# One kernel, 116 small stages in a new order: projections first, the last inverse by quarters, weights*v in two halves, u regrouped on VectorE

## The chip, the cores and the metric

The kernel runs on one core of one Trainium2 chip. The metric is the device time of one execution in microseconds (us). Most executions of a kernel agree within about 1.5%. A run that is over 1.5% above the fastest of its kernel counts as slow; such runs are left out of the comparisons. Two sets of numbers appear: the times of repeated runs, and the profile of one run of each kernel, whose span is about 2 us shorter than its time.

## The reference, cut to what matters

Two independent parts share the core; their outputs stand side by side.

```python
def _A_ref(x, wqkv, wo):                       # part A: sliding dilated attention, S=2048, D=640
    qkv = (x @ wqkv)...                        # q, k, v; 32 heads of 20
    idx = pos[:, None] - 2 * arange(8)         # each position sees 8 earlier ones, step 2
    logits = einsum("bhsd,bhswd->bhsw", q, kg) * scale
    attn = softmax(logits)
    o = einsum("bhsw,bhswd->bhsd", attn, vg)   # weights * v
    return o @ wo
def _B_ref(u, A, B, C, log_dt, Dskip):         # part B: a long convolution, L=2048, D=640, N=192
    P = exp(dt * A * l)                        # powers; K is their sum over N
    K = einsum("dn,dnl,dn->dl", C, P, dt * B).real
    y = irfft(rfft(u, 2L) * rfft(K, 2L))[:L]   # one transform per channel
    return y + u * Dskip
return concatenate([a, b], axis=-1)            # the bodies are abridged
```

## The kernel before

The stages, with the letters that the change gives them: `q k v` are the projections (five slices each, of 20 matmuls), `L` the logits of one half of a block of 512 positions, `N` the softmax normalisation, `A` weights*v for one of five slices, `O` the output projection. For part B, `G` makes the generators (sines and cosines) of the powers, `M` one of five tables with the convolution kernel made of it, `U` regroups u, `f g x y` are an FFT (u's first step, the table's first step, the second step with the product, the transform back), `S` the skip product, and `I` the last inverse. `R` frees the projections' memory and opens the FFT's.

```python
ORDER = "L0 V0 M1 F0 L1 M2 F1 V1 L2 M3 F2 V2 M4 F3 L3 F4 S012 I012 V3 S34 I34"

# in front of ORDER, fixed: generators, table 0, k, q, u, v
gens(tc, pools, ta, wi, 0, 1, dst0, done0); batch(1, 3); batch(3, 5)
make(0)
for ct in range(5): a.proj("k", ct)
for ct in range(5): a.proj("q", ct)
for i in range(4):
    us = att.tile([128, 16, 160], bf16, name="us", tag="p2")            # one buffer
    ... four loads on the GpSimd queue
    for h in range(2):
        uc = att.tile([128, NCH, 8, 32], bf16, name="uc", tag="prod", bufs=2)
        nc.gpsimd.tensor_copy(out=uc[:], in_=us[:, 8*h:8*h+8].rearrange("p l (c t) -> p c l t", c=NCH))
        nc.gpsimd.dma_start(out=Ud[:, :, s]..., in_=uc[:]...)
for ct in range(5): a.proj("v", ct)

# one projection slice: TensorE into two PSUM buffers, ScalarE moves each out
for sc in range(4):
    ps = self.psp.tile([128, 512], f32, name="ps_p", tag="a", bufs=2)
    for kt in range(5): nc.tensor.matmul(ps[:], ...)
    nc.scalar.copy(out=st[:, sc], in_=ps[:])

# weights * v: one multiply, one buffer
p2 = p.tile([128, 2, 4, PB], bf16, name="p2", tag="p2")
V.tensor_tensor(out=p2[:], in0=windows(v...), in1=self.at[b][:]..., op=A.mult)
ps = self.psp.tile([128, PB], f32, name="ps_o", tag="l", bufs=2)
for u2 in range(2):
    for d in range(4):
        nc.tensor.matmul(ps[32*d:32*d+32], lhsT=G4, rhs=p2[:, u2, d], start=(u2 == 0), stop=(u2 == 1), ...)
# (cut: everything else)
```

The softmax here doesn't subtract the row's maximum and nothing guards it: scores larger than these inputs give would overflow.

## Time and profile before

459.38 us is the median of three runs (459.04 to 460.1).

The first lines of the page of the kernel before: the span; busy time of TensorE (PE), its weight loads, VectorE (DVE), ScalarE (ACT) and GpSimd (POOL); then the busy share of TensorE and VectorE, and the clock granted to TensorE, each in 40 slices of the span, in tenths.

```profile
span 457.8 us, 13032 instructions
...
PE 352.9 (77%) x5560; PEld 232.3 (51%) x5560; DVE 350.9 (77%) x521; ACT 253.6 (55%) x485; POOL 82.2 (18%) x149
...
PE   1863646196999766599898979988799799998680
...
DVE  1499947998799984568999798989889944576443
...
PEclk9999978878899965579998988999599978999896
```

No engine is full: the two busiest stand at 77%. Where they idle is told by the windows view. Each row is a stretch: from and to in us, its length, then busy us of PE, PEld, DVE, ACT, POOL, the granted clock, the DMA share and GB/s.

```profile
0.00:97.00 97.00, 49.09 (x222) 20.44 (x223) 72.22 (x159) 64.34 (x123) 36.36 (x62) 0.90 0.76 190
97.00:156.00 59.00, 55.07 (x716) 28.51 (x717) 54.08 (x96) 31.30 (x54) 7.13 (x10) 0.94 0.54 183
156.00:200.00 44.00, 27.24 (x669) 16.70 (x663) 27.49 (x27) 9.74 (x17) 8.81 (x23) 0.57 0.67 189
200.00:360.00 160.00, 146.69 (x2547) 108.78 (x2546) 144.40 (x185) 98.05 (x193) 15.13 (x30) 0.93 0.38 115
360.00:416.00 56.00, 49.01 (x1052) 37.59 (x1046) 35.86 (x39) 35.11 (x68) 4.40 (x8) 0.91 0.52 173
416.00:458.00 42.00, 25.81 (x372) 20.27 (x370) 16.80 (x20) 15.09 (x34) 10.33 (x16) 0.85 0.63 139
```

The middle (200 to 360) is about 91% full on both engines. At 156 to 200 both are near 62% at once, and the granted clock is 0.57. In that stretch VectorE, from 160.5 on, has only the first attention block to work on. Its timeline there (start, length, line, operation, output<-inputs; in brackets the idle time before it and what ended that) shows a chain that goes back and forth between the engines and the transfers:

```profile
174.15 0.96 DVE L448 RECIPROCAL rc<-ps_n 128x128 f32<-128x128 f32 x1 [4.48 <-PE ps_n L445]
...
179.69 1.22 DVE L456 TENSOR_TENSOR attn<-attn,ps_r 128x1024 bf16<-128x1024 bf16 x1 [3.98 <-PE ps_r L455]
...
184.39 2.29 DVE L467 TENSOR_TENSOR p_1859<-vb,attn 128x4096 bf16<-128x4096 bf16 x1 [1.15 <-PE ps_o L471]
189.19 2.29 DVE L467 TENSOR_TENSOR p_1876<-vb,attn 128x4096 bf16<-128x4096 bf16 x1 [2.51 <-DMA vb<-vd]
```

The waits of TensorE (who waited at which line, for whom; us in total, times, longest) show one large item: the projections wait 30.3 us for ScalarE, which is busy with the generators' sines.

```profile
PE ps_p L400 <- ACT st L401: 30.3, 8, 9.8
```

At the end, three pieces of the chain that ended last (start, length, what): the transform back ends at 423.5, and after it evictions, an output projection and a store follow one another up to 457.8.

```profile
424.12 3.08 ACT ysb L685 x8
...
432.56 4.27 PE ps_op L482 x20
...
442.63 5.10 DMA out_dram<-ud
```

### The profile page before, as it was taken

Reading aid. Unit: us, or ns where it says so; the run is one execution under the profiler, and the core shown is the slowest. Engines: PE = TensorE matmul, PEld = TensorE weight load, DVE = VectorE, ACT = ScalarE, POOL = GpSimd, SP = SyncE. Lnnn points to the kernel's source line nnn. Section 1 sums busy time; section 2 is a strip of 40 time slices with the busy share of each in tenths; the row PEclk is TensorE's granted clock in tenths of the full one; section 3 lists DMA queues with packets and bytes.
Section 4 is the critical chain, followed back from the end, with each engine's and each line's share of the span. In section 5 each row is a group of like instructions: output and inputs, shape, how many; then the busy total and the mean of one; then the engine's idle time right before and its main releaser. Section 6 shows DMA issues by size and latency. Waiting matters only on the chain.

```text
span 457.8 us, 13032 instructions
## 1 busy us (share of the span) xinstructions
PE 352.9 (77%) x5560; PEld 232.3 (51%) x5560; DVE 350.9 (77%) x521; ACT 253.6 (55%) x485; POOL 82.2 (18%) x149
## 2 busy tenths in 40 slices
PE   1863646196999766599898979988799799998680
PEld 0520212045444344166587737667476576776470
DVE  1499947998799984568999798989889944576443
ACT  1869646984455401176771775673276734786540
POOL 8235640000500020310000220000210000010232
PEclk9999978878899965579998988999599978999896
DMA  8999656435664293774051543241443108583687
GB/s 180 259 212 231 184 157 221 133 133 168 187 246 153 90 298 91 186 226 133 21 210 50 141 128 130 105 163 50 103 154 124 62 4 311 203 229 95 157 204 113
DMA packets 64822, 71.50 MB, mean 156 GB/s; under 512 B 29744, under 2 KB 55664, under 8 KB 63868
## 3 DMA queue, kind: packets, MB, share of 16 engines
q1 hardware_dynamic: 57740, 54.89, 40.6%
q0 software_dynamic: 5664, 14.96, 13.0%
q10 hardware_dynamic: 1360, 0.82, 0.7%
q8 instruction: 43, 0.70, 0.7%
q14 instruction: 15, 0.12, 0.1%
HBM read 43.72 MB, written 24.02 MB: 148 GB/s over the span
## 4 chain that ended last, share of the span: by engine, by line
PE 37%; DVE 11%; ACT 6%; issue 3%; DMA 2%; POOL 0%; DVEq 0%; POOLq 0%; ACTq 0%
PE ps_ia L351 9%; PE ps_k L280 7%; PE ps_op L482 4%; PE ps_s L304 3%; ACT S L338 3%; PE ps_o L471 3%; DVE Yf L341 2%; PE ps_l L436 1%; DVE krtmp L223 1%; ACT ysb L685 1%; DMA vb<-vd 1%; DVE Ytab L223 1%; DMA out_dram<-ud 1%; DVE prod L434 1%; PE ps_r L455 1%
## 5 line engine op out<-in xcount | busy, mean ns | idle before, releaser
L400 PE MATMUL ps_p<-xT,w_309 128*128 128x512 bf16 x100 | 36.2, 526 | 35.9 <-ACT st L401 30.3
L434 DVE TENSOR_TENSOR prod<-qb,kb 128x2048 bf16<-128x2048 bf16 x40 | 47.5, 1221 | 19.1 <-PE ps_l L436 17.2
L280 PE MATMUL ps_k<-Ytab,Xtab 128*20 128x33 bf16 (+1 forms) x2560 | 51.9, 245 | 11.9 <-issue 10.6
L465 POOL DMA_DIRECT2D vb<-vd x40 | 22.2, 558 | 201.8 <-DVE p_4181 L467 43.8
L280 PEld LDWEIGHTS <-Xtab 128*20 128x20 bf16 (+1 forms) x2560 | 45.5, 126 | 20.8 <-issue 18.0
L401 ACT CAST st<-ps_p 128x512 bf16<-128x512 f32 x60 | 34.7, 580 | 24.7 <-PE ps_p L400 24.2
L400 PEld LDWEIGHTS <-w_309 128*128 128x128 bf16 x100 | 12.1, 123 | 59.2 <-issue 50.6
L351 PE MATMUL ps_ia<-cEA,Yf 128*128 128x256 bf16 x320 | 41.0, 295 | 0.2 <-DVE Yf L341 0.2
L351 PEld LDWEIGHTS <-Yf 128*128 128x128 bf16 x320 | 33.3, 106 | 9.3 <-DVE Yf L341 3.3
L353 ACT CAST Z<-ps_ia 128x512 bf16<-128x512 f32 x40 | 23.4, 585 | 22.7 <-PE ps_ia L351 22.6
L482 PE MATMUL ps_op<-wo,oT 128*128 128x320 bf16 x160 | 30.1, 322 | 5.3 <-ACT oT L473 4.0
L223 DVE TENSOR_TENSOR Ytab<-Ytab 128x2688 bf16<-128x2688 bf16 (+3 forms) x25 | 30.7, 1228 | 2.4 <-DMA Ytab<-Gdram 2.1
L336 PEld LDWEIGHTS <-cT 128*64 128x64 bf16 x640 | 22.9, 113 | 16.2 <-issue 14.4
L223 DVE TENSOR_TENSOR krtmp<-Ytab 128x2688 bf16<-128x2688 bf16 (+3 forms) x25 | 29.7, 1190 | 0.2
L282 ACT CAST Kd<-ps_k 128x363 bf16<-128x363 f32 (+1 forms) x15 | 6.8, 453 | 40.8 <-PE ps_k L280 40.8
L341 DVE TENSOR_TENSOR Yf<-S 128x1024 bf16<-128x1024 bf16 x40 | 25.7, 687 | 3.4 <-ACT S L338 3.4
L223 DVE TENSOR_TENSOR krtmp<-Xtab,Xg 128x768 bf16<-128x768 bf16 (+2 forms) x40 | 26.2, 655 | 0.6
L223 DVE TENSOR_TENSOR Xtab<-Xtab,Xg 128x768 bf16<-128x768 bf16 (+2 forms) x40 | 25.7, 650 | 0.3
L214 ACT ACTIVATE cs<-ph 128x768 bf16<-128x768 int32 x22 | 17.7, 842 | 13.0 <-DMA Gdram<-cs 13.0
L400 PE MATMUL ps_p<-xT,w_311 128*128 128x512 bf16 x100 | 24.5, 406 | 0.0
L436 PE MATMUL ps_l<-prod,cGs 128*32 128x512 bf16 x160 | 18.9, 424 | 7.1 <-DVE prod L434 7.1
L482 PEld LDWEIGHTS <-oT 128*128 128x128 bf16 x160 | 14.6, 101 | 18.9 <-ACT oT L473 10.5
(452 smaller groups left out, 745.6 us busy)
## 6 DMA issues: line engine op xcount, KB each, us to landing
vb<-vd SPq DMA_DIRECT2D x40, 128.5 KB, 3.0
vb<-vd POOLq DMA_DIRECT2D x40, 128.5 KB, 3.7
Gdram<-cs SPq DMA_DIRECT2D x24, 192.0 KB, 3.8
HB<-k_HB SPq DMA_DIRECT2D x2, 2048.0 KB, 8.4
kb<-kd SPq DMA_DIRECT2D x4, 657.5 KB
us<-in_B_u_dram POOLq DMA_DIRECT2D x16, 160.0 KB, 6.2
Udram<-uc POOLq DMA_DIRECT2D x8, 320.0 KB, 5.0
kd<-st SPq DMA_DIRECT2D x5, 512.0 KB, 3.8
```

The source lines that it names most:

```text
L223: V.tensor_tensor(out=o[0], in0=Y[0], in1=gr, op=A.mult)
L280: MM(ps[32 * g:32 * g + 20, i, :], lhsT=X[rows, part % 2, :, col + t0 + i], rhs=Y[rows, :, part % 2, col + t0 + i], start=(part == 0 and i ...
L336: nc.tensor.matmul(ps[64 * dd:64 * dd + 64, kk, r], lhsT=T[:, k, r, :], rhs=A1[:, k, :, 64 * dd:64 * dd + 64], start=(kk == 0 and r == 0), ...
L341: V.tensor_tensor(out=Yf[:, 2 * i:2 * i + 2, :, 32 * b:32 * b + 32], in0=K, in1=u.unsqueeze(1).to_broadcast([128, 2, 16, 32]), op=A.mult)
L351: nc.tensor.matmul(ps[:, jj].rearrange("p l r d -> p (l r d)"), lhsT=Yf[:, q, 2 * jq + jj, :], rhs=C["EA"][:, q, :], start=(jj == 0 and q ...
L353: nc.scalar.copy(out=Z[:, :, :, 4 * jq:4 * jq + 4].rearrange("p l r (j d) -> p (l r) j d", d=2), in_=ps[:].rearrange("p j l r d -> p (l r) ...
L400: nc.tensor.matmul(ps[:], lhsT=w[:, kt, 128 * ct:128 * ct + 128], rhs=self.xT[:, kt, 512 * sc:512 * sc + 512], start=(kt == 0), stop=(kt = ...
L401: nc.scalar.copy(out=st[:, sc], in_=ps[:])
L434: V.tensor_tensor(out=pr[:], in0=q[:, ct].unsqueeze(1).to_broadcast([128, 4, PB]), in1=windows(k[:, ct, 2 * u2:2 * u2 + PB], 4, 4), op=A.mult)
L436: nc.tensor.matmul(ps[32 * g:32 * g + 32], lhsT=C["Gs"][:, ct, :], rhs=pr[:, g, :], start=(ct == 0), stop=(ct == 4), tile_position=(0, 32 ...
L465: (nc.sync if g % 2 else nc.gpsimd).dma_start(out=v[32 * g:32 * g + 32], in_=self.vd[:, 4 * dg:4 * dg + 4, PB * b + 4 * g:PB * b + 4 * g + ...
L482: nc.tensor.matmul(ps[:], lhsT=self.oT[b][:, t, 128 * x:128 * x + 128], rhs=self.wo_sb[:, t, 320 * eh:320 * eh + 320], start=(t == 0), sto ...
```

## The change

The intent is to fill idle time. No matmul and no eviction is removed. (1) The coarse stages become 116 small ones, and the written order is new: q and k first, the fixed front dissolved, the eight pieces of the last inverse (four quarters for each of two batches) spread over the tail. (2) weights*v becomes two multiplies of half the size in two buffers, so that TensorE can start on the first half. (3) The eight copies that regroup u go from GpSimd to VectorE, and u's tile is halved and gets two buffers. Core of the diff, with the mere splitting of functions into stages cut:

```diff
-ORDER = "L0 V0 M1 F0 L1 M2 F1 V1 L2 M3 F2 V2 M4 F3 L3 F4 S012 I012 V3 S34 I34"
+ORDER = "q4 q1 q2 q3 q0 G0 G1 k0 k4 k2 v4 k1 k3 M0 U1 U0 v2 U2 U4 v0 v3 U5 U7 U6 v1 L0 L1 U3 N0
+         A0 A1 A2 A3 A4 G3 R0 L2 L3 N1 M1 O2 O1 O0 O3 f0 g0 x0 f1 A5 M2 A6 A7 g1 y0 x1 M3 A8 A9
+         ... f4 A15 A16 A17 A18 A19 g4 x4 I0 I1 S4 S5 y4 I2 S6 I4 I3 S7 O13 O14 I5 O12 I6 O15 I7"
...
-        p2 = p.tile([128, 2, 4, PB], bf16, name="p2", tag="p2")
-        V.tensor_tensor(out=p2[:], in0=windows(v[:, :, 0:PB], 2, 2), in1=..., op=A.mult)
         for u2 in range(2):
+            p2 = p.tile([128, 4, PB], bf16, name="p2", tag="p2", bufs=2)
+            V.tensor_tensor(out=p2[:], in0=v[:, :, 2 * u2:2 * u2 + PB], in1=..., op=A.mult)
...
-        us = att.tile([128, 16, 160], bf16, name="us", tag="p2")
+        us = att.tile([128, 8, 160], bf16, name="us", tag="p2", bufs=2)
...
-            nc.gpsimd.tensor_copy(out=uc[:], in_=us[:, 8 * h:8 * h + 8].rearrange("p l (c t) -> p c l t", c=NCH))
+        V.tensor_copy(out=uc[:], in_=us[:].rearrange("p l (c t) -> p c l t", c=NCH))
```

More of the change, by code (lines that the diff above doesn't have):

```diff
@@ L19 @@
 CW = 192
-ORDER = "L0 V0 M1 F0 L1 M2 F1 V1 L2 M3 F2 V2 M4 F3 L3 F4 S012 I012 V3 S34 I34"
+ORDER = "q4 q1 q2 q3 q0 G0 G1 k0 k4 k2 v4 k1 k3 M0 U1 U0 v2 U2 U4 v0 v3 U5 U7 U6 v1 L0 L1 U3 N0 A0 A1 A2 A3 A4 G3 R0 L2 L3 N1 M1 O2 O1 O0 O3 f0 g0 x0 f1 A5 M2 A6 A7 g1 y0 x1 M3 A8 A9 O6 O5 O7 L4 L5 N2 y1 O4 f2 g2 x2 M4 S0 S1 S2 S3 A10 A11 y2 f3 g3 A12 A13 A14 O9 O11 x3 O8 y3 L6 O10 L7 N3 f4 A15 A16 A17 A18 A19 g4 x4 I0 I1 S4 S5 y4 I2 S6 I4 I3 S7 O13 O14 I5 O12 I6 O15 I7"
 MAGIC = 12582912.0
@@ L118, in partB_prep @@
     W = NCH * CW
-    nat01 = ap.tile([128, 4, NCH, CW], bf16, name="nat01", tag="p2")
-    nat2 = ap.tile([128, 2, NCH, CW], bf16, name="nat2", tag="prod", bufs=2)
-    nat = [nat01[:, a] for a in range(4)] + [nat2[:, a] for a in range(2)]
+    nat = []
+    for tag in ("p2", "p2", "prod"):
+        nt = ap.tile([128, 2, NCH, CW], bf16, name="nat", tag=tag, bufs=2)
+        nat += [nt[:, 0], nt[:, 1]]
     ldt = pp.tile([128, NCH], bf16, name="ldt")
@@ L420, in load_wo, with logits @@
             nc.gpsimd.dma_start(out=self.wo_sb[32 * q:32 * q + 32], in_=src[q])
-    def logits(self, b):
+    def logits(self, b, u2):
         nc, V, p, C = self.nc, self.nc.vector, self.p, self.pools
-        q = p.tile([128, 5, PB], bf16, name="qb", tag="qb")
-        k = p.tile([128, 5, HALO + PB], bf16, name="kb", tag="kb")
-        nc.sync.dma_start(out=q[:], in_=self.qd[:, :, PB * b:PB * b + PB])
-        nc.sync.dma_start(out=k[:], in_=self.kd[:, :, PB * b:PB * b + PB + HALO])
-        self.at[b] = at = p.tile([128, 2, PB], bf16, name="attn", tag="attn")
-        for u2 in range(2):
-            ps = self.psp.tile([128, PB], f32, name="ps_l", tag="l", bufs=2)
-            for ct in range(5):
-                pr = p.tile([128, 4, PB], bf16, name="prod", tag="prod", bufs=2)
-                V.tensor_tensor(out=pr[:], in0=q[:, ct].unsqueeze(1).to_broadcast([128, 4, PB]), in1=windows(k[:, ct, 2 * u2:2 * u2 + PB], 4, 4), op=A.mult)
-                for g in range(4):
-                    nc.tensor.matmul(ps[32 * g:32 * g + 32], lhsT=C["Gs"][:, ct, :], rhs=pr[:, g, :],
-                                     start=(ct == 0), stop=(ct == 4), tile_position=(0, 32 * g), skip_group_check=True)
-            nc.scalar.activation(out=at[:, u2, :], in_=ps[:], func=ACT.Exp, scale=SCALE)
@@ new lines, in logits @@
+        if u2 == 0:
+            q = p.tile([128, 5, PB], bf16, name="qb", tag="qb")
+            k = p.tile([128, 5, HALO + PB], bf16, name="kb", tag="kb")
+            nc.sync.dma_start(out=q[:], in_=self.qd[:, :, PB * b:PB * b + PB])
+            nc.sync.dma_start(out=k[:], in_=self.kd[:, :, PB * b:PB * b + PB + HALO])
+            self.qk = q, k
+            self.at[b] = p.tile([128, 2, PB], bf16, name="attn", tag="attn")
+        q, k = self.qk
+        at = self.at[b]
+        ps = self.psp.tile([128, PB], f32, name="ps_l", tag="l", bufs=2)
@@ new lines, in logits @@
+        for ct in range(5):
+            pr = p.tile([128, 4, PB], bf16, name="prod", tag="prod", bufs=2)
+            V.tensor_tensor(out=pr[:], in0=q[:, ct].unsqueeze(1).to_broadcast([128, 4, PB]), in1=windows(k[:, ct, 2 * u2:2 * u2 + PB], 4, 4), op=A.mult)
+            for g in range(4):
+                nc.tensor.matmul(ps[32 * g:32 * g + 32], lhsT=C["Gs"][:, ct, :], rhs=pr[:, g, :],
+                                 start=(ct == 0), stop=(ct == 4), tile_position=(0, 32 * g), skip_group_check=True)
@@ L439, in logits, with norm @@
+        nc.scalar.activation(out=at[:, u2, :], in_=ps[:], func=ACT.Exp, scale=SCALE)
+    def norm(self, b):
+        nc, V, p, C = self.nc, self.nc.vector, self.p, self.pools
+        at = self.at[b]
         if b == 0:
@@ L465, in av, with out_proj @@
             (nc.sync if g % 2 else nc.gpsimd).dma_start(out=v[32 * g:32 * g + 32], in_=self.vd[:, 4 * dg:4 * dg + 4, PB * b + 4 * g:PB * b + 4 * g + PB + 2])
-        p2 = p.tile([128, 2, 4, PB], bf16, name="p2", tag="p2")
-        V.tensor_tensor(out=p2[:], in0=windows(v[:, :, 0:PB], 2, 2), in1=self.at[b][:].unsqueeze(2).to_broadcast([128, 2, 4, PB]), op=A.mult)
         ps = self.psp.tile([128, PB], f32, name="ps_o", tag="l", bufs=2)
         for u2 in range(2):
+            p2 = p.tile([128, 4, PB], bf16, name="p2", tag="p2", bufs=2)
+            V.tensor_tensor(out=p2[:], in0=v[:, :, 2 * u2:2 * u2 + PB], in1=self.at[b][:, u2].unsqueeze(1).to_broadcast([128, 4, PB]), op=A.mult)
             for d in range(4):
-                nc.tensor.matmul(ps[32 * d:32 * d + 32], lhsT=self.pools["G4"][:], rhs=p2[:, u2, d], start=(u2 == 0), stop=(u2 == 1),
+                nc.tensor.matmul(ps[32 * d:32 * d + 32], lhsT=self.pools["G4"][:], rhs=p2[:, d], start=(u2 == 0), stop=(u2 == 1),
                                  tile_position=(0, 32 * d), skip_group_check=True)
         nc.scalar.copy(out=self.oT[b][:, dg], in_=ps[:])
-    def out_proj(self, b):
+    def out_proj(self, b, x):
         nc, p = self.nc, self.p
-        for x in range(4):
-            ob = p.tile([128, D], bf16, name="ob", tag="ob", bufs=2)
-            for eh in range(2):
-                ps = self.psp.tile([128, 320], f32, name="ps_op", tag="a", bufs=2)
-                for t in range(5):
-                    nc.tensor.matmul(ps[:], lhsT=self.oT[b][:, t, 128 * x:128 * x + 128], rhs=self.wo_sb[:, t, 320 * eh:320 * eh + 320], start=(t == 0), stop=(t == 4))
-                nc.scalar.copy(out=ob[:, 320 * eh:320 * eh + 320], in_=ps[:])
-            p0 = PB * b + 128 * x
-            nc.sync.dma_start(out=self.out[p0:p0 + 128, :], in_=ob[:])
+        ob = p.tile([128, D], bf16, name="ob", tag="ob", bufs=2)
+        for eh in range(2):
+            ps = self.psp.tile([128, 320], f32, name="ps_op", tag="a", bufs=2)
+            for t in range(5):
+                nc.tensor.matmul(ps[:], lhsT=self.oT[b][:, t, 128 * x:128 * x + 128], rhs=self.wo_sb[:, t, 320 * eh:320 * eh + 320], start=(t == 0), stop=(t == 4))
+            nc.scalar.copy(out=ob[:, 320 * eh:320 * eh + 320], in_=ps[:])
+        p0 = PB * b + 128 * x
+        nc.sync.dma_start(out=self.out[p0:p0 + 128, :], in_=ob[:])
 def flat(ap):
@@ L599, in batch, with u_load @@
         gens(tc, pools, ta, wi, ca, cb, None, done)
-    gens(tc, pools, ta, wi, 0, 1, dst0, done0)
-    batch(1, 3)
-    batch(3, 5)
-    make(0)
-    for ct in range(5):
-        a.proj("k", ct)
-    for ct in range(5):
-        a.proj("q", ct)
-    for i in range(4):
-        us = att.tile([128, 16, 160], bf16, name="us", tag="p2")
-        s = slice(16 * i, 16 * i + 16)
+    def u_load(i):
+        us = att.tile([128, 8, 160], bf16, name="us", tag="p2", bufs=2)
+        s = slice(8 * i, 8 * i + 8)
@@ L612 @@
         for g in range(4):
             nc.gpsimd.dma_start(out=us[32 * g:32 * g + 32], in_=usrc[g, :, s])
-        for h in range(2):
-            uc = att.tile([128, NCH, 8, 32], bf16, name="uc", tag="prod", bufs=2)
-            s = slice(16 * i + 8 * h, 16 * i + 8 * h + 8)
-            nc.gpsimd.tensor_copy(out=uc[:], in_=us[:, 8 * h:8 * h + 8].rearrange("p l (c t) -> p c l t", c=NCH))
-            nc.gpsimd.dma_start(out=Ud[:, :, s].rearrange("c p l t -> p c (l t)"), in_=uc[:].rearrange("p c l t -> p c (l t)"))
@@ L619 @@
-    for ct in range(5):
-        a.proj("v", ct)
-    pools["prep"].release()
-    xw.release()
-    pools["fft"] = fp = sb("fft")
-    const(fp, "SEL", selm.reshape(128, -1), [128, nsel, 128], nc.sync)
-    const(fp, "T", cn["T"], [128, 32, 2, 64], nc.sync)
-    a.load_wo()
-    Z = fp.tile([128, 2, 64, 2, 32], bf16, name="Z")
-    inv = {}
-    def F(c):
+        uc = att.tile([128, NCH, 8, 32], bf16, name="uc", tag="prod", bufs=2)
+        V.tensor_copy(out=uc[:], in_=us[:].rearrange("p l (c t) -> p c l t", c=NCH))
@@ new lines, in u_load, with open_fft, spec_u @@
+        nc.gpsimd.dma_start(out=Ud[:, :, s].rearrange("c p l t -> p c (l t)"), in_=uc[:].rearrange("p c l t -> p c (l t)"))
+    inv, cur = {}, {}
+    def open_fft():
+        pools["prep"].release()
+        xw.release()
+        pools["fft"] = fp = sb("fft")
+        const(fp, "SEL", selm.reshape(128, -1), [128, nsel, 128], nc.sync)
+        const(fp, "T", cn["T"], [128, 32, 2, 64], nc.sync)
+        a.load_wo()
+        cur["Z"] = fp.tile([128, 2, 64, 2, 32], bf16, name="Z")
+    def spec_u(c):
+        fp = pools["fft"]
@@ L633, in F, with spec_k @@
         U = fp.tile([128, 64, 32], bf16, name="U", tag="UK")
         nc.sync.dma_start(out=U[:], in_=Ud[c])
-        A1 = fp.tile([128, 32, 2, 128], bf16, name="A1", tag="A1")
-        f1(tc, pools, C, (lambda t: U[:, :, t]), A1, 0)
-        K = fp.tile([128, 64, 32], bf16, name="K", tag="UK")
+        cur["A1"] = fp.tile([128, 32, 2, 128], bf16, name="A1", tag="A1")
+        f1(tc, pools, C, (lambda t: U[:, :, t]), cur["A1"], 0)
+    def spec_k(c):
+        K = pools["fft"].tile([128, 64, 32], bf16, name="K", tag="UK")
@@ L638, in F, with spec_x, back @@
         spread(tc, pools, C, Kds[c], K)
-        f1(tc, pools, C, (lambda t: K[:, :, t]), A1, 1)
-        Yf = fp.tile([128, 4, 16, 128], bf16, name="Yf", tag="Yf")
-        f2_prod(tc, pools, C, A1, Yf)
-        ia(tc, pools, C, Yf, Z[:, (c + 1) % 2])
+        f1(tc, pools, C, (lambda t: K[:, :, t]), cur["A1"], 1)
+    def spec_x(c):
+        cur["Yf"] = pools["fft"].tile([128, 4, 16, 128], bf16, name="Yf", tag="Yf")
+        f2_prod(tc, pools, C, cur["A1"], cur["Yf"])
+    def back(c):
+        Z = cur["Z"]
+        ia(tc, pools, C, cur["Yf"], Z[:, (c + 1) % 2])
@@ L651, in open_inv, with skip @@
             nc.sync.dma_start(out=HB[:, 32 * q:32 * q + 32].rearrange("p l r n -> p l (r n)"), in_=hsrc[:, 32 * q:32 * q + 32])
-    def skip(cs):
+    def skip(cs, q):
         ip, n = inv["p"], len(cs)
-        for q in range(4):
-            s = slice(16 * q, 16 * q + 16)
-            uq = ip.tile([128, n, 16, 32], bf16, name="uq", tag="uq", bufs=2)
-            nc.sync.dma_start(out=uq[:].rearrange("p c l t -> p c (l t)"), in_=Ud[cs[0]:cs[-1] + 1, :, s].rearrange("c p l t -> p c (l t)"))
-            inv[q] = ud = ip.tile([128, 16, n, 32], bf16, name="ud", tag="ud", bufs=4)
-            dv = Dsb[:, 32 * cs[0]:32 * cs[-1] + 32].rearrange("p (c t) -> p c t", t=32).unsqueeze(1).to_broadcast([128, 16, n, 32])
-            V.tensor_tensor(out=ud[:], in0=uq[:].rearrange("p c l t -> p l c t"), in1=dv, op=A.mult)
@@ L664, in inverse @@
-    def inverse(cs):
-        ip, n = inv["p"], len(cs)
-        per = 512 // (32 * n) // 4 * 4
-        for q in range(4):
-            s = slice(16 * q, 16 * q + 16)
+        s = slice(16 * q, 16 * q + 16)
+        uq = ip.tile([128, n, 16, 32], bf16, name="uq", tag="uq", bufs=2)
+        nc.sync.dma_start(out=uq[:].rearrange("p c l t -> p c (l t)"), in_=Ud[cs[0]:cs[-1] + 1, :, s].rearrange("c p l t -> p c (l t)"))
+        inv[n, q] = ud = ip.tile([128, 16, n, 32], bf16, name="ud", tag="ud", bufs=4)
@@ new lines, in skip, with inverse @@
+        dv = Dsb[:, 32 * cs[0]:32 * cs[-1] + 32].rearrange("p (c t) -> p c t", t=32).unsqueeze(1).to_broadcast([128, 16, n, 32])
+        V.tensor_tensor(out=ud[:], in0=uq[:].rearrange("p c l t -> p l c t"), in1=dv, op=A.mult)
+    def inverse(cs, q):
+        ip, n, Z = inv["p"], len(cs), cur["Z"]
+        per = 512 // (32 * n) // 4 * 4
+        s = slice(16 * q, 16 * q + 16)
+        if n == 3:
+            z = ip.tile([128, 3, 16, 2, 32], bf16, name="zq", tag="zq", bufs=2)
+            for i in range(3):
+                nc.sync.dma_start(out=z[:, i], in_=Zd[i][:, s])
+            ysb = ip.tile([128, 16, n, 32], bf16, name="ysb", tag="ysb", bufs=2)
+        else:
+            z = Z[:, :, s]
+        ud = inv[n, q]
+        for o in range(0, 16, per):
+            ps = psp.tile([128, per, n, 32], f32, name="ps_ib", tag="b", bufs=3)
+            for i in range(per):
+                for r in range(2):
+                    nc.tensor.matmul(ps[:, i], lhsT=inv["HB"][:, 16 * q + o + i, r, :], rhs=z[:, :, o + i, r, :], start=(i == 0 and r == 0), stop=(r == 1), skip_group_check=True)
@@ L670, in inverse @@
             if n == 3:
-                z = ip.tile([128, 3, 16, 2, 32], bf16, name="zq", tag="zq", bufs=2)
-                for i in range(3):
-                    nc.sync.dma_start(out=z[:, i], in_=Zd[i][:, s])
-            else:
-                z = Z[:, :, s]
-            ud = inv[q]
-            if n == 3:
-                ysb = ip.tile([128, 16, n, 32], bf16, name="ysb", tag="ysb", bufs=2)
-            for o in range(0, 16, per):
-                ps = psp.tile([128, per, n, 32], f32, name="ps_ib", tag="b", bufs=3)
-                for i in range(per):
-                    for r in range(2):
-                        nc.tensor.matmul(ps[:, i], lhsT=inv["HB"][:, 16 * q + o + i, r, :], rhs=z[:, :, o + i, r, :], start=(i == 0 and r == 0), stop=(r == 1), skip_group_check=True)
-                if n == 3:
-                    nc.scalar.copy(out=ysb[:, o:o + per], in_=ps[:])
-                else:
-                    V.tensor_tensor(out=ud[:, o:o + per], in0=ps[:], in1=ud[:, o:o + per], op=A.add)
@@ L688, in inverse @@
-            if n == 3:
-                V.tensor_tensor(out=ud[:], in0=ud[:], in1=ysb[:], op=A.add)
-            for g in range(4):
-                (nc.sync if g < 2 else nc.gpsimd).dma_start(out=dst_b[g, :, s, 32 * cs[0]:32 * cs[-1] + 32], in_=ud[32 * g:32 * g + 32].rearrange("p l c t -> p l (c t)"))
-    def V_(b):
-        for dg in range(5):
-            a.av(b, dg)
-        a.out_proj(b)
-    for st in ORDER.split():
-        op, x = st[0], st[1:]
-        if op == "F":
-            F(int(x))
-        elif op == "M":
-            make(int(x))
-            if x == "4":
-                open_inv()
-        elif op == "L":
-            a.logits(int(x))
-        elif op == "V":
-            V_(int(x))
-        elif op == "S":
-            skip([int(i) for i in x])
-        elif op == "I":
-            inverse([int(i) for i in x])
@@ L714, with make_ @@
-    ip = inv["p"]
+                nc.scalar.copy(out=ysb[:, o:o + per], in_=ps[:])
+            else:
+                V.tensor_tensor(out=ud[:, o:o + per], in0=ps[:], in1=ud[:, o:o + per], op=A.add)
+        if n == 3:
+            V.tensor_tensor(out=ud[:], in0=ud[:], in1=ysb[:], op=A.add)
+        for g in range(4):
+            (nc.sync if g < 2 else nc.gpsimd).dma_start(out=dst_b[g, :, s, 32 * cs[0]:32 * cs[-1] + 32], in_=ud[32 * g:32 * g + 32].rearrange("p l c t -> p l (c t)"))
+    def make_(c):
+        make(c)
+        if c == NCH - 1:
+            open_inv()
@@ new lines @@
+    batches = {3: (0, 1, 2), 2: (3, 4)}
+    stages = {
+        "G": lambda c: gens(tc, pools, ta, wi, 0, 1, dst0, done0) if c == 0 else batch(c, c + 2),
+        "M": make_,
+        "k": lambda ct: a.proj("k", ct),
+        "q": lambda ct: a.proj("q", ct),
+        "v": lambda ct: a.proj("v", ct),
+        "U": u_load,
+        "R": lambda _: open_fft(),
+        "L": lambda i: a.logits(i // 2, i % 2),
+        "N": a.norm,
+        "A": lambda i: a.av(i // 5, i % 5),
+        "O": lambda i: a.out_proj(i // 4, i % 4),
+        "f": spec_u,
+        "g": spec_k,
+        "x": spec_x,
+        "y": back,
+        "S": lambda i: skip(batches[3 - i // 4], i % 4),
+        "I": lambda i: inverse(batches[3 - i // 4], i % 4),
+    }
@@ L715 @@
+    for st in ORDER.split():
+        stages[st[0]](int(st[1:]))
+    ip, fp = inv["p"], pools["fft"]
     fp.release()
```

## The prediction

> **What bounds it now.** No single engine: the page gives TensorE 352.9 and VectorE 350.9 us busy of 457.8 (77% each). The windows view shows where both idle:
>
> | stretch us | PE busy | DVE busy | what |
> |---|---|---|---|
> | 0-97 | 49.1 | 72.2 | set-up, table 0, k projections in pieces |
> | 97-156 | 55.1 | 54.1 | table 0's matmuls, q and v projections |
> | 156-200 | 27.2 | 27.5 | attention block 0 alone; granted clock 0.57 |
> | 200-360 | 146.7 | 144.4 | FFT stages, attention, tables |
> | 360-416 | 49.0 | 35.9 | last FFTs |
> | 416-458 | 25.8 | 16.8 | inverse, attention 3, stores |
>
> 200-360 is about 91% full. The time to win is at 0-97 (waits view: projections wait 30.3 us for ScalarE's evictions), 156-200, and after 416. At 156-200 the timeline shows a chain: block 0's products end at 169.7, VectorE waits 4.5 and 4.0 us for the normalisation's matmuls, then 1.2 to 2.5 us before each of four weights*v multiplies (for the DMA of v or PE). The first FFT matmul comes at 193.9.
>
> **What changes**, by the program order of the changed kernel:
> - All q and k and one v slice precede table 0's matmuls. Twenty projection matmuls take 4.42 us. After table 0 (about 98 us again; VectorE decides it) 4 v slices are left, 18 us instead of 41: projections end at about 128 instead of 155.8.
> - Block 0's attention stands on VectorE among table 1 and generator instructions. At the trace's mean durations VectorE has about 66 us between table 0 and the first FFT matmul: about 165 instead of 194. Table 1's matmuls (about 10 us of PE) and three weights*v come later. Net lead about 14 us.
> - 20 multiplies of 2.29 us become 40; products of that output size take 1.22 us: +3 us of VectorE, and up to 3 us of waits saved by two buffers.
> - u's eight copies leave GpSimd (1.25 to 2.72 us each) for VectorE: estimate 0.75 us each, +6. In exchange VectorE no longer stalls beside them: while two ran, at 47.6-50.4 us, its 384-element shifts took 1.41 us instead of 0.35. The Trainium skill, "SBUF — State Buffer" (Who interferes with whom), says that GpSimd and VectorE block each other on shared ports; the trace agrees. I take these as cancelling.
> - Tail: two inverse quarters precede the last back-transform. Before, 25 us pass from its end (423.4) to the last matmul (448.2). After, I count about 14 us of matmuls there, with waits 16 to 18: about 8 us less. The final 9 us stay.
>
> No matmul or eviction is removed; the gain is idle time.
>
> **Sum.** 459.4 - 14 - 8 - 2 = about 436 us, range 424 to 450. Chances: faster by over 2% 0.88, within 2% 0.10, slower 0.02.
>
> **What would show it.** First FFT matmul at 160-175 us; projections over by about 130; VectorE within 8 us of 351 busy, TensorE within 10 of 353, both near 81%; GpSimd copies gone; granted clock above 0.88, no hole at 156-200; last back-transform to last matmul under 19 us.
>
> **What would make it wrong.** (a) ScalarE has 20 more evictions among the generators before table 0: if VectorE waits longer for its sines than the 11.3 us of before, table 0 slips. (b) The in-order transfer queue puts q, k, v stores between generator stores; a 5 us stall at 57-62 us already comes of such a wait. (c) DMA is busy 0.94 to 1.08 in the first 40 us; q's weights now come early there. (d) The middle, 91% full, gives back what the start gained.

## More of the kernel before

A list scheduler of the programming framework places the instructions of each engine: the order in which stages are written gives the priority, and an instruction that is ready may overtake one that is not. So a change of the written order, and also a change of one instruction, moves thousands of others.

## The result, and the profile after

The changed kernel took 428.28 us (median of four runs, 426.9 to 430.95) against 459.21 us (458.48 to 460.1) of the kernel before on the same chip. Ratios here and below are the mean time of one kernel's fast runs over the mean of the other's fast runs of the same rounds, so not quite the ratio of the quoted medians: 0.9333, with a 95% interval of 0.9284 to 0.9381. It is faster by 6.7%.

The page after, the same lines as before:

```profile
span 425.1 us, 13065 instructions
...
PE 342.8 (81%) x5551; PEld 229.8 (54%) x5560; DVE 345.7 (81%) x549; ACT 252.1 (59%) x485; POOL 80.2 (19%) x157
...
PE   0496977899695259999999899858899889999962
...
DVE  0469999999789998998999888999889924489261
...
PEclk9997999999598559999999869975899986999995
```

Both busy times fell a little (VectorE's although eight copies of 0.82 us were added to it), and their shares rose to 81%. Of the 32.7 us by which the span fell, TensorE's idle time gave 22.6 (104.9 to 82.3): most of the gain is idle time, as intended. The other 10.1 us are busy time of the same matmuls; the mean granted clock rose from 0.879 to 0.896 in these two profiles, and how much of the 10.1 us that explains was not isolated. (Busy time is a union, in which records of neighbouring instructions overlap. Added up one by one, VectorE's durations rose from 382.9 to 386.3 us.) The windows view after, cut at its own stages:

```profile
0.00:95.00 95.00, 66.38 (x333) 29.96 (x339) 72.94 (x166) 68.27 (x135) 36.44 (x71) 0.96 0.86 225
95.00:130.00 35.00, 30.40 (x597) 17.09 (x599) 30.60 (x64) 24.46 (x41) 4.24 (x8) 0.85 0.66 211
130.00:156.00 26.00, 8.73 (x71) 2.95 (x70) 26.00 (x27) 3.65 (x5) 5.07 (x15) 0.61 0.80 253
156.00:200.00 44.00, 41.68 (x905) 29.57 (x902) 40.14 (x55) 24.28 (x48) 7.96 (x16) 0.96 0.53 150
200.00:340.00 140.00, 126.26 (x2386) 96.39 (x2384) 131.91 (x189) 85.92 (x167) 11.84 (x24) 0.90 0.33 103
340.00:389.00 49.00, 44.51 (x908) 34.10 (x900) 27.96 (x31) 29.54 (x57) 4.39 (x8) 0.90 0.59 198
389.00:426.00 37.00, 24.88 (x370) 19.70 (x368) 16.19 (x23) 16.02 (x36) 10.31 (x16) 0.86 0.69 147
```

Up to 95 us TensorE now does 66.4 us of work where it did 49.1 up to 97. The stretch in which both engines idled is gone. What is left of it is a hole of TensorE alone: at 130 to 156 it works 8.73 of 26 us, at a granted clock of 0.61, while VectorE works 26.00 of 26. Since VectorE is full there, that hole looks harmless; experiment e7 tries to fill it.

The projections' wait for ScalarE shrank from 30.3 to 9.4 us:

```profile
PE ps_p L401 <- ACT st L402: 9.4, 10, 2.4
```

Block 0's normalisation and multiplies, in VectorE's timeline after, run without a wait, with table 1's instructions between them (one is shown):

```profile
143.94 0.96 DVE L457 RECIPROCAL rc<-ps_n 128x128 f32<-128x128 f32 x1
...
148.29 1.22 DVE L465 TENSOR_TENSOR attn<-attn,ps_r 128x1024 bf16<-128x1024 bf16 x1
149.42 1.56 DVE L224 TENSOR_TENSOR krtmp<-Ytab 128x2688 bf16<-128x2688 bf16 x1
150.89 1.23 DVE L478 TENSOR_TENSOR p_1737<-vb,attn 128x2048 bf16<-128x2048 bf16 x1
```

The tail, in three pieces of the chain that ended last:

```profile
395.69 7.42 DMA out_dram<-ud
...
411.87 4.95 DMA out_dram<-ob
...
417.40 2.84 PE ps_op L491 x10
```

Milestones of the two profiles, read from TensorE's timeline (us):

| milestone | before | after | lead |
|---|---|---|---|
| projections end | 155.9 | 130.2 | 25.7 |
| first FFT matmul | 193.9 | 155.6 | 38.3 |
| second transform back ends | 283.4 | 259.7 | 23.7 |
| last transform back ends | 423.5 | 400.8 | 22.7 |
| last matmul | 448.2 | 420.2 | 28.0 |
| end of span | 457.8 | 425.1 | 32.7 |

The lead at the first FFT matmul is partly borrowed (table 1 and some weights*v come later), so the lead at the second transform back is the fair measure of the start: 23.7 us. The middle gives back 1.0 us, and the tail adds 10.0 us.

### The profile page after: what moved, and what is told of

It is laid out like the page before. It is cut to its first block, busy times and chain, and to the rows that moved or that the text cites. A ratio compares the mean times of both kernels' runs of the same rounds, so it can differ in the third digit from the quotient of the medians.

```text
span 425.1 us, 13065 instructions
## 1 busy us (share of the span) xinstructions
PE 342.8 (81%) x5551; PEld 229.8 (54%) x5560; DVE 345.7 (81%) x549; ACT 252.1 (59%) x485; POOL 80.2 (19%) x157
## 4 chain that ended last, share of the span: by engine, by line
PE 42%; DVE 8%; ACT 6%; issue 3%; DMA 3%; SPq 1%; POOL 0%; DVEq 0%; ACTq 0%
PE ps_k L281 9%; PE ps_ia L352 8%; PE ps_op L491 5%; ACT S L339 4%; PE ps_s L305 3%; PE ps_o L480 3%; PE ps_l L440 2%; DMA out_dram<-ud 2%; DVE krtmp L224 1%; DMA out_dram<-ob 1%; DVE Yf L342 1%; DVE Ytab L224 1%; ACT oT L482 1%; DVE Ytab L226 0%; ACT A_6832 L320 0%
## 5 line engine op out<-in xcount | busy, mean ns | idle before, releaser
L281 PEld LDWEIGHTS <-Xtab 128*20 128x20 bf16 (+1 forms) x2560 | 45.1, 126 | 22.6 <-issue 19.9
L352 PE MATMUL ps_ia<-cEA,Yf 128*128 128x256 bf16 x320 | 40.1, 287 | 0.0
L352 PEld LDWEIGHTS <-Yf 128*128 128x128 bf16 x320 | 32.1, 103 | 7.8 <-issue 1.6
L401 PE MATMUL ps_p<-xT,w_312 128*128 128x512 bf16 x98 | 27.6, 433 | 7.3 <-ACT st L402 4.7
L337 PEld LDWEIGHTS <-cT 128*64 128x64 bf16 x640 | 23.7, 115 | 15.6 <-issue 13.6
L224 DVE TENSOR_TENSOR Ytab<-Ytab 128x2688 bf16<-128x2688 bf16 (+3 forms) x25 | 29.8, 1193 | 0.1
L401 PE MATMUL ps_p<-xT,w_310 128*128 128x512 bf16 x97 | 22.7, 378 | 3.8 <-ACT st L402 3.5
L482 ACT CAST oT<-ps_o 128x512 bf16<-128x512 f32 x20 | 12.0, 598 | 22.8 <-PE ps_o L480 22.6
L401 PE MATMUL ps_p<-xT,w_314 128*128 128x512 bf16 x96 | 23.8, 399 | 1.8 <-ACT st L402 1.2
L224 DVE TENSOR_TENSOR krtmp<-Xtab,Xg 128x768 bf16<-128x768 bf16 (+2 forms) x40 | 25.2, 629 | 0.1
L492 ACT CAST ob<-ps_op 128x320 bf16<-128x320 f32 x32 | 13.1, 430 | 18.3 <-DMA out_dram<-ob 9.7
```

What stands on the lines that cost most here:

```text
L224: V.tensor_tensor(out=o[0], in0=Y[0], in1=gr, op=A.mult)
L281: MM(ps[32 * g:32 * g + 20, i, :], lhsT=X[rows, part % 2, :, col + t0 + i], rhs=Y[rows, :, part % 2, col + t0 + i], start=(part == 0 and i ...
L337: nc.tensor.matmul(ps[64 * dd:64 * dd + 64, kk, r], lhsT=T[:, k, r, :], rhs=A1[:, k, :, 64 * dd:64 * dd + 64], start=(kk == 0 and r == 0), ...
L352: nc.tensor.matmul(ps[:, jj].rearrange("p l r d -> p (l r d)"), lhsT=Yf[:, q, 2 * jq + jj, :], rhs=C["EA"][:, q, :], start=(jj == 0 and q ...
L401: nc.tensor.matmul(ps[:], lhsT=w[:, kt, 128 * ct:128 * ct + 128], rhs=self.xT[:, kt, 512 * sc:512 * sc + 512], start=(kt == 0), stop=(kt = ...
```

## The experiments

Theory T: the order makes most of the gain; at the front by filling ScalarE's and VectorE's idle time, at the end by spreading the inverse. The prediction had counted the two edits of instructions as nearly nothing, above all u's copies "as cancelling". Rivals: the edits do it and the order little; or the order needs the edits.

Where the ratios of two runs are subtracted below, both intervals count: such a difference is uncertain by 0.6 to 1 point, which is 3 to 5 us. Milestones come from one profile of each kernel. In the rounds of f1 to f4, one run of the kernel before (465.54 us) counts as slow.

### e1: the changed code in the old order

```diff
-ORDER = "q4 q1 q2 ..."
+ORDER = "G0 G1 G3 M0 k0..k4 q0..q4 U0..U7 v0..v4 R0 L0 L1 N0 A0..A4 O0..O3 M1 f0 g0 x0 y0 ..."
```

> The changed kernel with its stages in the old order; the halves of weights*v and u on VectorE stay. Theory A (the order alone fills idle time of TensorE and VectorE): 452 to 460 us, as before the change. Rival B (the two new buffers of weights*v and the copies taken off GpSimd remove the waits): at most 440 us.

Measured: 454.14 us (450.96 to 456.14); ratio to the kernel before 0.9898 (0.982 to 0.9977). In this order the two edits are worth 1%. The time lies in Theory A's range, but it says nothing of the order alone: the new order without the edits was not run. The projections wait for ScalarE 29.6 us and end at 153.9, the first FFT matmul is at 188.9. The other 5.7 points of the gain appear only with the new order.

### e4 and e5: one half of the order alone

e4 has the new order up to `f0` and the old one after it; e5 has the old front and the new rest.

> New order up to the first FFT, old order after it. Theory A with my split (start worth about 22 us by the milestones of the trace, middle and tail about 9): 434 to 441 us, first FFT matmul at about 155 us. Rival C (the order after the first FFT does most, the early lead is given back in the full middle): at least 447 us.

> The old order up to block 0's attention, then the new order. Theory X: the two parts of the order add up. From the run with the old order (454.1) the front alone won 11.3 us (442.9) and the rest after it 14.6 (428.3), so the rest alone gives 437 to 442 us. Rival Y: the rest pays only when the front has moved the first FFT matmul forward; then 447 us or more, and the first FFT matmul stays at 185 to 195 us.

Measured: e4 442.88 us, ratio 0.9662 (0.959 to 0.9734), which lies between the two ranges. e5 461.21 us, ratio 1.0035 (0.9968 to 1.0102); that is in Rival Y's range, the first FFT matmul (196.1) 1.1 us beyond it. Against e1's 0.9898, the front alone wins 2.4 points, the rest alone loses 1.4, both together win 5.7. The parts do not add up. e4's second transform back ends at 259.6, like the changed kernel's 259.7, but its third ends at 316.2 (309.6 after) and its last at 409.1 (400.8); its profiled run was the slowest of its four (445.04). So the new front makes the early lead, and the new rest keeps it; without the lead the new rest is worth nothing. Why it costs time there was not pursued.

### e2: u's copies back on GpSimd, ordered anew

```diff
-        V.tensor_copy(out=uc[:], in_=us[:].rearrange(...))
+        nc.gpsimd.tensor_copy(out=uc[:], in_=us[:].rearrange(...))
```

> The changed kernel with u's eight copies back on GpSimd. My prediction took the two sides of that move as cancelling (VectorE loses 8 x 0.82 us of copies, gets back stalls beside GpSimd): 426 to 433 us. Rival B: the copies on GpSimd cost 8 us or more, at least 436 us.

Measured: 438.11 us (437.49 to 439.4), ratio 0.9565 (0.9488 to 0.9641). This is 2.3 points, or 10.7 us of 459, worse than the change, though VectorE is rid of eight copies. Rival B's range holds, so the prediction's "cancelling" looks wrong; f1 decides.

### e9: an extra copy on GpSimd that nobody needs, ordered anew

```diff
         V.tensor_copy(out=uc[:], in_=us[:].rearrange(...))
+        du = cst.tile([128, NCH, 8, 32], bf16, name="du", tag="du")
+        nc.gpsimd.tensor_copy(out=du[:], in_=us[:].rearrange(...))
```

> The changed kernel, with u's copies on VectorE as they are, and beside each a second copy of the same tile on GpSimd into a scratch tile that nobody reads. It separates two reasons why the run with u's copies on GpSimd lost 10 us. Theory P: a running GpSimd copy slows VectorE's instructions that run beside it; then the dummies cost nearly as much: 434 to 440 us, the first FFT matmul at 160 or later, and single 384-element instructions of VectorE over 1 us between 20 and 95 us. Rival Q: what cost the time was that u's own path was longer (copy of 2.1 us in place of 0.8, in a queue with transfers); then dummies cost little: 426 to 431 us, first FFT matmul within 2 us of 155.6.

Measured: 434.91 us (433.38 to 437.2), ratio 0.9475 (0.9411 to 0.9539); first FFT matmul at 159.9. The time is in Theory P's range, the first FFT matmul 0.1 us short of it, and only one 384-element instruction took over 1 us at 20 to 95 us (1.42, at 62.2). Work on GpSimd whose result nobody reads costs 1.4 points.

There is a flaw in e2 and e9. The scheduler orders everything anew after each edit: in the profile of e9, 88 of VectorE's 541 instructions other than the copies stand elsewhere in its list than in the change. The new order may have been picked for exactly this program, so perhaps any disturbance costs 10 us. Four of the next runs, f1 to f4, remove that flaw. They hold every engine's instructions in exactly the order of the changed kernel, by ordering edges between consecutive instructions of an engine:

```diff
+def hold_order(tc, nc):                       # called after all stages are written
+    for engine, ranks in FROZEN.items():      # the changed kernel's order, by rank of writing
+        chain = [traced[engine][r] for r in ranks]
+        for a, b in zip(chain, chain[1:]):
+            tc.add_manual_dep(b, a.name, ...NoSync...)   # order only, no wait
```

Built with no other edit (not run on the chip), this gave the changed kernel's order back on all five engines. In the profiles of f1, f2 and f4 below, the lists of VectorE, ScalarE and GpSimd match the change's, the added or moved copies aside. Holding costs little by itself: in f4, whose edits concern the tail, the first FFT matmul is at 156.6 (155.6 in the change) and the last transform back ends at 403.2 (400.8).

### f1: u's copies on GpSimd, order held

> The changed kernel with u's eight copies on GpSimd again, but with every engine's instructions held in exactly the order of the changed kernel by ordering edges; each copy stands on GpSimd just before the store of its tile. The earlier run with the copies on GpSimd (ratio 0.9565, 10 us over the changed kernel) let the scheduler order everything anew, so it could not say whether the copies or the new order cost the time. Theory P (the copies' own doing): 433 to 440 us, first FFT matmul at 160 or later. Rival S (the disturbed order): 426 to 431 us, first FFT matmul within 2 us of 155.6.

Measured: 439.57 us (436.23 to 441.4), ratio 0.9548 (0.9503 to 0.9593); the first FFT matmul at 169.3. Theory P holds, and e2 is confirmed: the copies' own doing is 0.9548 - 0.9333 = 2.15 points, which is 9.9 us of 459. The loss arises early: table 0's matmuls start at 106.7 (95.7 in the change), and the second transform back ends at 272.8 (259.7). The eight copies took 17.5 us on GpSimd, 2192 ns each; on VectorE they take 818 ns. GpSimd makes them as soon as it can: seven of the eight pieces of u are stored 8.6 to 27.6 us earlier than in the change, and only the last one later (issued at 156.0, against 140.9).

### f2: dummy copies on GpSimd, order held

> The changed kernel in its exact order of instructions, u's copies on VectorE, with a second, unread copy of each tile of u on GpSimd (16 to 20 us of GpSimd work). Theory P1 (a GpSimd copy slows VectorE's instructions beside it, and this decides): 432 to 437 us, VectorE busy 3 to 6 us above 345.7. Rival P2 (slowing is small; what costs is that u comes later when GpSimd copies it): 427 to 430 us. Rival S (only a new order costs): 426 to 430 us, also here.

Measured: 435.98 us (433.98 to 437.24), ratio 0.9478 (0.9446 to 0.951). VectorE was busy 353.7 us, 8.0 more than in the change, with exactly the same instructions. P1's time holds, and its 3 to 6 us more of VectorE were passed: the dummies cost 1.45 points, 6.7 us, by the total times two thirds of f1's loss. Paired one by one with the change's, eight VectorE instructions grew by over 0.3 us, 8.0 us in all, 6.7 of them before table 0's matmuls. At the milestones f2 explains less of f1: table 0's matmuls start 3.0 us later than in the change (f1: 11.0), the first FFT matmul comes 5.2 later (13.7), the second transform back ends 6.3 later (13.1). The dummies also stand before u's stores in GpSimd's queue, and these leave up to 5.6 us later; that this adds to the loss is not excluded.

Two of the dummies in GpSimd's timeline of f2:

```profile
45.12 6.74 POOL L619 COPY du<-us 128x1280 bf16<-128x1280 bf16 x1
53.27 1.26 POOL L619 COPY du<-us 128x1280 bf16<-128x1280 bf16 x1
```

VectorE's timeline of f2 beside the second of them:

```profile
52.30 0.36 DVE L225 TENSOR_TENSOR Xtab<-Xtab,krtmp 128x384 bf16<-128x384 bf16 x1
52.58 2.18 DVE L226 TENSOR_TENSOR Xtab<-Xtab,krtmp 128x384 bf16<-128x384 bf16 x1
54.79 0.96 DVE L224 TENSOR_TENSOR Xtab<-Xtab,Xg 128x1536 bf16<-128x1536 bf16 x1
```

and the same three instructions in the changed kernel:

```profile
51.40 0.36 DVE L225 TENSOR_TENSOR Xtab<-Xtab,krtmp 128x384 bf16<-128x384 bf16 x1
51.67 0.35 DVE L226 TENSOR_TENSOR Xtab<-Xtab,krtmp 128x384 bf16<-128x384 bf16 x1
52.06 0.96 DVE L224 TENSOR_TENSOR Xtab<-Xtab,Xg 128x1536 bf16<-128x1536 bf16 x1
```

The instruction at L226 took 2.18 us in place of 0.35, while the GpSimd copy recorded at 53.27 took 1.26 us (starts on GpSimd are recorded roughly); a copy with no VectorE instruction beside it took 1.25 us in the kernel before, at 61.5. The other copy, at 45.12, took 6.74 us while VectorE ran back to back: there GpSimd was the one that waited. The Trainium skill, "SBUF — State Buffer" (Who interferes with whom), says that VectorE and GpSimd share one pair of ports under an exclusive lock, that a VectorE instruction with two SBUF inputs contends with a GpSimd instruction that reads SBUF, and that the loser stops entirely. The trace agrees: one or the other stands still, and neither runs at half speed. A VectorE instruction with one input stood as well: the shift at L213 took 1.80 us in place of 0.36 beside the copy at 91.88.

What the rest of f1's loss is (3 us by the total times, more by the milestones) was not isolated. The profile offers candidates: the last piece of u arrives later, VectorE's waits for ScalarE's sines grow from 5.4 to 11.4 us, and copies and transfer starts stand in line on one engine.

### e3 and f3: weights*v joined to one multiply again

```diff
         for u2 in range(2):
-            p2 = p.tile([128, 4, PB], bf16, name="p2", tag="p2", bufs=2)
-            V.tensor_tensor(out=p2[:], in0=v[:, :, 2*u2:2*u2+PB], ...)
+        p2 = p.tile([128, 2, 4, PB], bf16, name="p2", tag="p2")      # one multiply, one buffer
+        V.tensor_tensor(out=p2[:], in0=windows(v...), ...)
-        us = att.tile([128, 8, 160], bf16, name="us", tag="p2", bufs=2)
+        us = att.tile([128, 8, 160], bf16, name="us", tag="us")      # forced: p2 has no second buffer
```

e3 was ordered anew, f3 held the order of the change. The set-up's tile nat, which shares the buffer, goes back to its old form in both.

> The changed kernel with weights*v as one multiply into one buffer, as before the change (u then loads into one buffer of its own, because the shared space is gone). Theory A: 428 to 433 us, a few waits of 1 to 2 us come back at weights*v. Rival B: at least 436 us.

> The changed kernel in its exact order, with each pair of weights*v multiplies joined to one again (one buffer), standing at the place of the first half; u's pieces use one buffer of their own. The earlier run of this (ratio 0.9526) was ordered anew. Theory: the split's gain is the overlap of the second half with TensorE; joined, VectorE is 3 us less busy but waits for the one buffer: 429 to 434 us, and VectorE's waits for TensorE before the multiplies rise by 5 us or more in all. Rival: the split is worth nothing by itself and the earlier loss was the disturbed order: 425 to 428.5 us.

Measured: e3 432.96, 438.16 and 439.21 us, and one run of 486.26 us, slow, which was the profiled one (granted clock 0.657) and is not read here; ratio of the fast runs 0.9526 (0.9427 to 0.9625), in Rival B's range. f3 442.54 us (440.04 to 443.98), ratio 0.9616 (0.9579 to 0.9653). In the order of the change, the edit costs 2.8 points, 13 us, more than either theory expected. Three lines of f3's waits:

```profile
DVE p L477 <- PE ps_o L480: 12.4, 7, 3.3
...
PE ps_o L480 <- DVE p L477: 11.1, 9, 5.4
...
DVE uc L617 <- DMA us<-in_B_u_dram: 9.0, 2, 5.7
```

With two buffers and the same order (f4 below), the first of these is 3.5 us and the second 5.3 us. So the ping-pong between VectorE and TensorE that the split was to remove does come back. But the third line is a confound: the joined tile left no second buffer for u, and VectorE waits 9.0 us for u's loads. The profile allots it: the first FFT matmul comes 9.4 us later than in the change, and the last matmul 16.5 us later, so some 9 us may belong to u's buffer, and about 7 to the joined multiply. That division is read from one profile, whose 16.5 us are more than the 13 us of the total times, and was not tested by a run of its own.

### e7: the first FFT earlier, to fill TensorE's hole

```diff
-... U5 U7 U6 v1 L0 L1 U3 N0 A0 A1 A2 A3 A4 G3 R0 L2 L3 N1 M1 O2 O1 O0 O3 f0 g0 x0 ...
+... U5 U7 U6 U3 v1 G3 R0 f0 L0 L1 N0 g0 A0 A1 A2 A3 A4 L2 L3 N1 M1 O2 O1 O0 O3 x0 ...
```

> The changed kernel, with the last copied piece of u moved before the last v slice and the first FFT stage (u's transform, then the spread and the table's transform) moved before block 0's attention, to fill TensorE's idle time at 130 to 160 us. Theory G: TensorE work done in that hole is missing later, where TensorE bounds: first FFT matmul at 135 to 148, total 420 to 426 us. Rival H: VectorE is busy without a break from 95 to 220 us and decides; TensorE merely waits elsewhere: 427 to 431 us though the first FFT matmul comes 8 us or more earlier.

Measured: 439.61 us (434.8 to 440.98), ratio 0.9554 (0.9478 to 0.9631). Both theories missed, though the first FFT matmul came at 145.2 as meant. Like e2 and e9, e7 was ordered anew, and its profiled run is its fastest (434.8). Two lines of its waits at 136 to 182 us:

```profile
PEld L317 <- DMA U<-Udram: 3.7, 1, 3.7
PE ps_f L317 <- DMA U<-Udram: 3.5, 1, 3.5
```

and one of VectorE's timeline:

```profile
150.47 1.22 DVE L465 TENSOR_TENSOR attn<-attn,ps_r 128x1024 bf16<-128x1024 bf16 x1 [2.33 <-PE ps_r L464]
```

In the program's order, the small matmul that VectorE needed for the normalisation stood behind the first FFT matmuls, and TensorE waited 3.5 us for u to land before these. VectorE's busy time at 140 to 180 fell from 38.5 to 32.4 us. By 340 us VectorE had done 295.4 us of work; in the change, it had done 301.6. VectorE's lost work is the likely price of the filled hole: the lead of 10.4 us at the first FFT matmul is gone at the second transform back (263.6, against 259.7).

But that is not where e7 loses most. Its fourth transform back ends at 363.4 (363.2 in the change) and its last at 402.6 (400.8), its span at 432.7 (425.1): 5.8 of the 7.6 us between the two profiles are lost after the last transform back. There the chain goes through a load for the inverse:

```profile
410.83 5.00 DMA zq<-Zdram
```

So e7 shows that the filled hole brought nothing, and not that it cost 10 us: most of the loss in its profile arises in the tail, whose order the scheduler changed too. A run with the order of the tail held was not made.

### e8 and f4: buffers in the tail

e8 gives the output projection four output buffers (`ob`) in place of two. f4 does that with the order held, and also puts the first piece of the second skip product in a free buffer of another tile.

```diff
-        ob = p.tile([128, D], bf16, name="ob", tag="ob", bufs=2)
+        ob = p.tile([128, D], bf16, name="ob", tag="ob", bufs=4)
-        ud = ip.tile([128, 16, n, 32], bf16, name="ud", tag="ud", bufs=4)
+        ud = ip.tile([128, 16, n, 32], bf16, name="ud", tag="ysb" if (n, q) == (2, 0) else "ud", ...)   # f4 only
```

> The changed kernel with four output buffers of the output projection in place of two (ob). In the changed kernel the last output projection's matmuls wait 3 us for an eviction that waits for an earlier store. Theory: this wait is the end of the chain; 424 to 427 us, and last back-transform to last matmul under 17.5 us (19.4). Rival: the wait hides another one just behind it (the last inverse quarters on VectorE); 427 to 430 us.

> A candidate that should beat both kernels: the changed kernel in its exact order, with four output buffers of the output projection in place of two, and the first piece of the second skip product in a free buffer of another tile, so that VectorE does not wait 7.7 us at 396 to 403 us for the store of the first inverse quarter, and ScalarE not 8.4 us for an output store. Theory: these two waits are the tail's chain: 419 to 424 us, last back-transform to last matmul 14 to 17 us (19.4). Rival: the store queue is the limit of the tail (DMA 0.80 busy at 400 to 420 us): 426 to 429 us.

Measured: e8 429.83 us (427.14 to 434.88; the run of 434.88 counts as slow), ratio 0.9332 (0.9245 to 0.9419). f4 429.07 us (425.26 to 432.43; one run of 432.43 counts as slow), ratio 0.9316 (0.9268 to 0.9364). Neither can be told from the change's 0.9333, so the theories of both failed. The waits did go. In f4, 12.0 us pass from the last transform back (403.2) to the last matmul (415.2), where the change has 19.4. But then the end is set by the store after the last inverse quarters:

```profile
403.76 1.64 ACT ysb L693 x4
...
414.82 2.98 DMA out_dram<-ud
...
418.63 0.69 DVE ud L695
```

From the end of the last transform back to the end of the span f4 takes 22.7 us and the change 24.3. The wait was on the chain, with another one close behind. No run is clearly faster than the change.

**Order and edits together.** Theory T is not shown. The edits without the new order are worth 1.0 point (e1). Taken singly out of the new order, the copies cost 2.15 points (f1) and the joined multiply with u's single buffer 2.8 (f3). The corner that would decide, the new order with neither edit, was not run. If the two losses simply added up, it would stand at 0.9333 + 0.0215 + 0.0283 = 0.983: an estimate from these three runs, by which the order alone would be worth about 1.7 points of the 6.7. So the runs speak for the last rival: order and edits need each other.

## Why the prediction was right, and where it was wrong

The total was right: 436 us with 424 to 450 was predicted, 428.28 came, 7.7 us lower. It is right in part by luck: the sum credits the gain to the order and next to nothing to the two edits, and that the runs do not bear out. The terms of the sum fared as follows.

| step, as predicted | measured |
|---|---|
| start: net lead about 14 us | 23.7 us at the second transform back; 10.6 us with u's copies on GpSimd and the order held (f1: 283.4 - 272.8) |
| u's copies "cancelling", 0 | 9.9 us gained (f1); dummy copies alone cost 6.7 (f2) |
| multiplies: +3 us of work, up to 3 us of waits saved | 1.22 us each as predicted; worth more than that: 13 us with u's second buffer (f3), about 7 of it by f3's profile |
| middle may give back | 1.0 us given back |
| tail 8 us, "the final 9 us stay" | 10.0 us; 5.3 before the last matmul, 4.7 after it |

**The step that failed is "I take these as cancelling".** Its cost was sized well: 0.75 us per copy was estimated, 0.82 measured, 6.5 us in all. Its benefit was seen in the trace (instructions of 1.41 us in place of 0.35), and the right mechanism was named, but it was priced by a guess. The dummies of f2 stretch VectorE's work by 8.0 us. The copies of f1 do the same: VectorE is busy 347.6 us there, while the change without its own copies is 345.7 - 6.5 = 339.2, a stretch of 8.4 us. The benefit falls early, before the FFTs: table 0's matmuls start at 95.7 us, against 106.7 in f1, though only 98.7 with f2's standstills, so part of the early loss has another cause, and that stays open. With that term taken out, the prediction comes near: 436 predicted, 439.57 in f1. That closeness is partly luck, because the term of the multiplies was mis-sized too.

**The start went as described, and its lead was mis-sized.** The lead was 23.7 us and not 14. The projections were over at 130.2 (predicted about 130), table 0's matmuls began at 95.7 (about 98), and the first FFT matmul came at 155.6, before the range of 160 to 175, which it misses. Fear (a), that more evictions on ScalarE would make VectorE wait longer for its sines, did not come true: that wait fell from 11.3 to 5.4 us. Fear (b) was not tested by a run. The late transfer that the trace shows is of another kind: the load of u for the first FFT was issued only at 149.0, when the last piece of u had been stored; e7 shows that hurrying it did not pay. Fear (c), a DMA already full in the first 40 us, brought no harm that was seen: its share there was 1.01 before and is 0.94 now.

**"No hole at 156-200" was half right.** That stretch is full now (41.7 and 40.1 of 44 us), but TensorE has a hole at 130 to 156 instead. It is not a stretch in which both idle: e7 filled part of it and gained nothing. The Trainium skill, "TensorE: Matmul & The Clock Gate" (What's actually happening), says that the clock is halved after an idle window and restored by activity. The trace agrees in part. The windows view gives a clock of 0.50 from 169.2 to 199.9 us before and from 135.7 to 159.6 after (0.57 and 0.61 over the whole holes), and 0.96 at 156 to 200 now. But in those 30.7 us before, TensorE worked 19.6 and never stood for longer than 2.4 us at a time: half clock came there with sparse work, without a long idle stretch. The mean granted clock went from 0.879 to 0.896, above the 0.88 predicted.

**Busy times:** VectorE 345.7 (within 8 of 351, as predicted). TensorE 342.8, which misses "within 10 of 353" by 0.2. Both stand at 81%, as predicted.

**Tail:** "under 19 us" from the last transform back to the last matmul was 19.4, a narrow miss: the last output projection waited 3.1 us for an output buffer whose earlier store was still under way. The 9 us after the last matmul did not stay (4.9), because the last matmul is now an output projection and no longer an inverse quarter. e8 and f4 say why the split of these two numbers means little: what is taken from one comes back in the other.

**The middle** was feared as the place where the gain is given back. It kept all but 1.0 us, and e4 suggests that this is the work of the new rest of the order: with the new front and the old rest, the lead at the last transform back is 14.4 us (423.5 - 409.1) where the change has 22.7.

## What to carry to other kernels

Price a copy on GpSimd by what VectorE loses beside it, not by the idle time of GpSimd: here eight copies cost 8 us of VectorE's time, more than the 6.5 us that the copies themselves take there. Before filling a hole of one engine, look at the other busy engine in the same window: here it was full, and filling the hole brought nothing. When a scheduler reorders everything after each edit, hold the order before pricing one part of a change, run the order without the edits as well as the edits without the order, and expect the parts of an order not to add up (here 2.4 and -1.4 points make 5.7).

## What the Trainium skill lacked or had wrong

- "SBUF — State Buffer" (Who interferes with whom): it says that the engine that issues second stops until the first one's instruction is finished. In f2 a GpSimd copy that takes 1.26 us undisturbed took 6.74 us, through twelve VectorE instructions in a row. So GpSimd can lose to a whole run of instructions; the page speaks of one.
- "SBUF — State Buffer", same section: it has no price for a whole kernel. Here eight copies of 128x1280 bf16 stretched VectorE's work by 8.0 us (f2) and 8.4 us (f1), one us per copy.
- "GPSIMD Engine Reference" (8. Key points): it says that VectorE is about 2 times faster for elementwise work. Its section 4.1 limits this to instructions with two inputs and calls GpSimd roughly line-rate with one. For this copy, which has one input, the factor is 1.5 undisturbed (1.26 against 0.82 us), between the two, and 2.7 with VectorE at work beside it (2192 against 818 ns).
